# A decode step of attention and gMLP: the last K pair loaded in two pieces, and x's load placed after the first Exp in the program's text

## The chip, the cores and the metric

The kernel runs on one core of one Trainium2 chip. Its time is the device time of one execution in microseconds (us). "The span" is the profile's time from the first to the last instruction of one execution; the run time is 1.7 to 2.2 us longer, because it includes what happens before and after.

The engines have short names: PE multiplies matrices, DVE and ACT do vector and scalar work, and SP here does nothing but issue DMAs (copies between device memory and on-chip memory). Sixteen DMA engines share each large copy. A DMA reports its landing on a semaphore, a counter that other engines can wait for.

## The reference, cut to what matters

One token, batch 1, all arrays bf16. The first part is attention with layer norm and a residual, and the second is a gated MLP with layer norm and a residual.

```python
q = layernorm(x) @ wq                      # 640 -> 32 heads x 192
k, v = the last 4096 keys of k_cache, v_cache   # 32 heads, 192 each: 2 x 50 MB
p = softmax(q . k * 192 ** -0.5)           # per head
h = x + (p @ v) @ wo                       # 6144 -> 640
z = gelu(layernorm(h) @ w_in)              # 640 -> 1536
z1, z2 = z[:768], layernorm(z[768:])
out = h + (z1 * (w_sp * z2 + b_sp)) @ w_out    # 768 -> 640
```

Nearly all of the 119 MB that must be read are K and V. The arithmetic is small, so this is a kernel for streaming memory.

## The kernel before

SP issues all large loads in the order of a plan, into six buffers of 3 MB, as soon as a buffer is free. Each K or V load is one pair of heads; there are 16 pairs. The very last K pair and V pair come in four pieces, so that work on them can begin before all has landed.

```python
def dma_pair(kind, cache, t_):
    t = kvp.tile([P, KVE], BF16, tag="kv", name=kind + "_t")
    cuts = LAST if t_ == NP - 1 else (0, J)    # LAST = (0, J/2, 3J/4, 7J/8, J)
    for a, b in zip(cuts, cuts[1:]):
        load(t[:, None, a * Dh:b * Dh], pair_keys(cache, t_, a, b))
...                                            # the plan: wq, K, V, the last wo, w_in, w_out
nc.scalar.dma_start(out=x_row[:], in_=A_x[0])  # x, on ACT's queue
issue()                                        # wq and the first K loads, on SP's queue
nc.scalar.dma_start(out=wsp_bf[:, 0:1], ...)   # w_sp, two bytes
nc.scalar.dma_start(out=wsp_bf[:, 1:2], ...)   # b_sp, two bytes
nc.scalar.activation(out=warm[:], in_=warm[:], func=ACT.Exp)   # brings in the Exp table
...
```

The end of the program:

```python
project(NQ - 2, oT)                            # the last wo tile but one
...
values(NP - 1, vt, 0, LAST[-3])                # last V pair: 64 small matmuls, in pieces
fold(rows_sb)
values(NP - 1, vt, LAST[-3], LAST[-2])
...
values(NP - 1, vt, LAST[-2], J)
scaled(NP - 1)                                 # "the last V cast": PSUM to SBUF
columns(oT, NQ - 1, 1)
project(NQ - 1, oT)                            # needs the last wo tile
nc.vector.tensor_scalar(out=h_pc[:], ...)      # "the h cast": h is complete
...                                            # layer norm, w_in, gelu, layer norm, gate, w_out
nc.vector.tensor_copy(out=o_sb[:], in_=orow)   # "the output cast"
nc.sync.dma_start(out=out[...], in_=o_sb[0::32, :])   # the store
```

The framework gives each DMA in turn the next of eight DMA semaphores, 0 to 7. A DMA is not issued until the one eight before it, on the same semaphore, has landed. At the end of the program, SP waits for all semaphores, two to a wait, in a fixed order.

Of the kernel before, what the change touches and what calls it, by code (L numbers as in the profile page):

```python
# [9 lines left out]
F32 = mybir.dt.float32  # L10
I32 = mybir.dt.int32
ALU = mybir.AluOpType
ACT = mybir.ActivationFunctionType
# [3 lines left out]
def kernel(  # L17
# [14 lines left out]
    nc = tc.nc  # L32
    P = nc.NUM_PARTITIONS
# [4 lines left out]
    J = W // HALF  # L38
# [6 lines left out]
    NP = H // 2  # L45
# [10 lines left out]
    def load(out, in_):  # L56
        eng = nc.sync
        eng.add_instruction(mybir.InstDMACopy(  # L58
            name=nc.get_next_instruction_name(), mode="Copy", queue="qSPDynamicHW",
            ins=eng.lower_ap_dma(in_, for_custom_bir_dma=True),  # L60
            outs=eng.lower_ap_dma(out, for_custom_bir_dma=True)))

    def pair_keys(cache, t, a, b):
        h0 = 4 * (t // 2) + t % 2
        k0 = Sk - W + a * HALF
        return cache[0, h0:h0 + 3:2, k0:k0 + (b - a) * HALF, :].rearrange("h (p j) d -> p h (j d)", p=HALF // 2)
# [7 lines left out]
    LAST = (0, J // 2, 3 * J // 4, 7 * J // 8, J)  # L74
# [8 lines left out]
    const = ctx.enter_context(tc.tile_pool(name="const", bufs=1))  # L83
# [22 lines left out]

    def dma_pair(kind, cache, t_):
        t = kvp.tile([P, KVE], BF16, tag="kv", name=kind + "_t")
        cuts = LAST if t_ == NP - 1 else (0, J)
        for a, b in zip(cuts, cuts[1:]):  # L110
            load(t[:, None, a * Dh:b * Dh], pair_keys(cache, t_, a, b))
        tiles[(kind, t_)] = t
# [12 lines left out]
    for t_ in range(2):  # L125
        plan.append(("kv", lambda t=t_: dma_pair("k", A_k_cache, t)))
    for t_ in range(NP):
        if t_ + 2 < NP:
            plan.append(("kv", lambda t=t_ + 2: dma_pair("k", A_k_cache, t)))
        if t_ % 2 == 1 and t_ < NP - 1:  # L130
            plan.append(("wo", lambda q=t_ // 2: dma_wo(q)))
        plan.append(("kv", lambda t=t_: dma_pair("v", A_v_cache, t)))
# [8 lines left out]
    def issue():  # L141
        while plan and live[plan[0][0]] < limit[plan[0][0]]:
            kind, go = plan.pop(0)
            live[kind] += 1
            go()

    def free(kind, n=1):
        live[kind] -= n
        issue()

    nc.scalar.dma_start(out=x_row[:], in_=A_x[0])
    issue()
    wsp_bf = const.tile([1, 2], BF16)
    nc.scalar.dma_start(out=wsp_bf[:, 0:1], in_=B_w_sp[0:1])
    nc.scalar.dma_start(out=wsp_bf[:, 1:2], in_=B_b_sp.rearrange("(o n) -> o n", o=1))

    warm = const.tile([P, 1], F32)
    nc.vector.memset(warm[:], 0.0)
    nc.scalar.activation(out=warm[:], in_=warm[:], func=ACT.Exp)
    ones_bf = const.tile([P, P], BF16)  # L160
    nc.vector.memset(ones_bf[:], 1.0)
    ones_f = const.tile([P, P], F32)
# [501 lines left out]
```

## Time and profile before

| | before |
|---|---|
| time, median of 3 runs (lowest to highest) | 286.69 us (286.62 to 286.86) |
| span of the profiled execution | 285.0 us |
| mean granted PE clock in it | 0.818 |
| main DMA queue, share of 16 engines | 97.7% |

The queue is the limit over the whole span.

The end of the chain of waits, in order of time (start, duration, what), says what ended last:

```profile
260.53 13.82 DMA wo_t<-in_A_wo_dram
...
280.97 1.01 PE sc_ps L632 x18
282.01 0.33 DVE o_sb L635
```

So the last wo tile, landing at 274.35, ends the streaming part, and small steps follow until the output cast at 282.01. The timeline of the same stretch (start, duration, engine, line, operation, and what ended the idle time before) has the last V pair's matmuls, the last V cast and the store:

```profile
269.52 1.60 PE L404 MATMUL pv_176<-v_t,E_125 128*2 128x192 bf16 x44
...
272.51 0.26 DVE L429 CAST ol_1866<-pv_176 128x96 bf16<-128x96 f32 x1 [0.33 <-PE pv_176 L404]
...
274.39 0.53 PE L480 MATMUL attn_ps<-o_1882,wo_t 128*128 128x1 bf16 x15 [0.23 <-DMA wo_t<-in_A_wo_dram]
...
282.36 0.63 SPq L636 DMA_DIRECT2D out_dram<-o_sb  x1
```

The start of the program, also from the timeline:

```profile
0.74 0.51 ACTq L151 DMA_DIRECT2D x_row<-in_A_x_dram  x1
...
1.89 1.28 ACT L159 ACT_TABLE_LOAD   x1 [1.89 <-issue]
...
2.17 0.29 PE L239 MATMUL sm_ps<-ones_bf,x_row 1*128 1x1 bf16 x5 [2.17 <-DMA x_row<-in_A_x_dram]
...
6.49 0.16 DVE L243 COPY x_pc<-sm_ps 128x5 f32<-128x5 f32 x1
```

x is issued at 0.74, PE has it at 2.17, and DVE takes the result only at 6.49, because it builds constants before. The wait list of SP has the wait for the store at the end of the program (in total, times, longest):

```profile
SPq L659 <- DMA out_dram<-o_sb: 0.9, 1, 0.9
```

### The profile page before, as it was taken

The numbers are of one execution on the slowest core, as the hardware profiler recorded it, in microseconds if no ns is written. First come the engines' busy times: TensorE is split into PE (matmuls) and PEld (weight loads), VectorE is DVE, ScalarE is ACT, GpSimd is POOL, SyncE is SP. The second block draws the span as 40 slices with busy tenths as digits, with TensorE's granted clock in tenths as the row PEclk, the third lists the DMA queues.
The fourth block names the chain that finished last, engine by engine and source line by source line (L and its number), as shares of the span: only waits on it lengthen the run. The fifth ranks groups of instructions, "written<-read, shape, count | busy, mean of one in ns | idle before, by whom it ended". The sixth has DMA issues, their size and how long they took to land.

```text
span 285.0 us, 3082 instructions
## 1 busy us (share of the span) xinstructions
PE 170.7 (60%) x1134; PEld 67.3 (24%) x1134; DVE 212.3 (74%) x289; ACT 64.1 (22%) x316; POOL 2.3 (1%) x10
## 2 busy tenths in 40 slices
PE   0329938474686259807772476535771876764864
PEld 0103413121132013302220122112320322321453
DVE  7300088989999995999699949996699849995343
ACT  2001237411441224014401440143101010202311
POOL 3000000000000000000000000000000000000000
PEclk9999996889599755985698759956896679999595
DMA  8999999999999999999999999999999998999993
GB/s 331 435 407 428 441 429 400 443 465 428 414 414 437 441 441 428 414 452 421 435 441 442 428 430 441 409 448 435 423 428 443 441 437 384 459 421 423 402 401 140
DMA packets 5565, 119.54 MB, mean 419 GB/s; under 512 B 1005, under 2 KB 2286, under 8 KB 2990
## 3 DMA queue, kind: packets, MB, share of 16 engines
q1 hardware_dynamic: 5544, 119.35, 97.7%
q8 instruction: 9, 0.15, 0.2%
q14 instruction: 6, 0.05, 0.0%
q10 hardware_dynamic: 6, 0.00, 0.0%
HBM read 119.34 MB, written 0.00 MB: 419 GB/s over the span
## 4 chain that ended last, share of the span: by engine, by line
DMA 40%; DVE 38%; PE 18%; issue 2%; SPq 1%; ACT 0%; DVEq 0%; ACTq 0%
DVE k_t L318 20%; DMA k_t<-in_A_k_cache_dram 20%; DMA v_t<-in_A_v_cache_dram 9%; PE sc_ps L325 8%; DMA wq_t<-in_A_wq_dram 6%; PE sc_ps L266 5%; DMA wo_t<-in_A_wo_dram 5%; DVE S L311 5%; DVE ob L439 4%; DVE S L332 3%; PE attn_ps L475 1%; SPq L58 1%; PE sm_ps L342 1%; DVE gm L344 1%; DVE m L335 1%
## 5 line engine op out<-in xcount | busy, mean ns | idle before, releaser
L325 PE MATMUL sc_ps<-k_t,ident_bf 128*128 128x512 bf16 x306 | 91.7, 459 | 45.6 <-DVE k_t L318 45.6
L318 DVE TENSOR_TENSOR k_t<-k_t,q_208 128x6144 bf16<-128x6144 bf16 x32 | 107.1, 3350 | 15.0 <-DMA k_t<-in_A_k_cache_dram 14.6
L325 PEld LDWEIGHTS <-ident_bf 128*128 128x128 bf16 x306 | 32.8, 112 | 96.0 <-issue 62.3
L308 ACT ACTIVATE k_t<-k_t 128x192 bf16<-128x192 bf16 x112 | 38.8, 347 | 34.1 <-DVE k_t L318 34.1
L332 DVE TENSOR_REDUCE S<-sc_ps 128x32 f32<-128x512 f32 (+1 forms) x32 | 21.8, 682 | 4.4 <-PE sc_ps L325 4.4
L266 PE MATMUL sc_ps<-wq_t,xn_128 128*128 128x512 bf16 x60 | 18.3, 467 | 10.3 <-DMA wq_t<-in_A_wq_dram 7.9
L308 ACT ACTIVATION_READ_ACCUMULATOR k_t<-k_t 128x1 f32 x112 | 20.9, 186 | 0.0
L311 DVE TENSOR_REDUCE S<-k_t 128x16 f32<-128x3072 bf16 x6 | 20.1, 3345 | 0.0
L274 DVE COPY sp_f<-sm_ps 128x2 f32<-128x2 f32 x1 | 0.2, 159 | 26.1 <-PE sm_ps L272 26.1
L361 ACT ACTIVATE E_125<-S,bias 128x64 bf16<-128x64 f32 x12 | 4.2, 360 | 46.3 <-DVE bias L351 46.3
L361 ACT ACTIVATE E_127<-S,bias 128x64 bf16<-128x64 f32 x10 | 3.5, 360 | 48.0 <-DVE bias L351 48.0
L361 ACT ACTIVATE E_126<-S,bias 128x64 bf16<-128x64 f32 x10 | 3.5, 362 | 42.9 <-DVE bias L351 42.9
L266 PEld LDWEIGHTS <-xn_128 128*128 128x128 bf16 x60 | 6.7, 112 | 21.6 <-issue 14.6
L268 ACT ACTIVATE q_208<-sc_ps 128x512 bf16<-128x512 f32 x6 | 3.6, 597 | 29.8 <-PE sc_ps L266 29.8
L344 DVE TENSOR_REDUCE gm<-sm_ps 2x1 f32<-2x128 f32 x16 | 4.5, 279 | 7.2 <-PE sm_ps L342 7.2
L414 PE MATMUL pv_174<-v_t,E_127 128*8 128x512 bf16 (+1 forms) x72 | 7.9, 489 | 3.1 <-DMA v_t<-in_A_v_cache_dram 3.1
L414 PE MATMUL pv_176<-v_t,E_126 128*8 128x512 bf16 (+1 forms) x72 | 7.3, 459 | 2.3 <-DMA v_t<-in_A_v_cache_dram 2.3
L414 PE MATMUL pv_176<-v_t,E_125 128*8 128x512 bf16 (+1 forms) x48 | 5.6, 509 | 1.1 <-DMA v_t<-in_A_v_cache_dram 1.1
L414 PE MATMUL pv_174<-v_t,E_125 128*8 128x512 bf16 (+1 forms) x72 | 6.2, 425 | 0.0
L414 PEld LDWEIGHTS <-E_127 128*8 128x8 bf16 (+1 forms) x120 | 3.4, 89 | 8.3 <-issue 6.4
L414 PEld LDWEIGHTS <-E_126 128*8 128x8 bf16 (+1 forms) x120 | 3.4, 86 | 7.6 <-issue 5.2
L414 PE MATMUL pv_176<-v_t,E_127 128*8 128x512 bf16 (+1 forms) x48 | 5.0, 472 | 0.2 <-DMA v_t<-in_A_v_cache_dram 0.2
(242 smaller groups left out, 148.4 us busy)
## 6 DMA issues: line engine op xcount, KB each, us to landing
k_t<-in_A_k_cache_dram SPq DMA_DIRECT2D x15, 3072.0 KB, 27.8
v_t<-in_A_v_cache_dram SPq DMA_DIRECT2D x15, 3072.0 KB, 30.6
wq_t<-in_A_wq_dram SPq DMA_DIRECT2D x5, 1536.0 KB, 14.1
wo_t<-in_A_wo_dram SPq DMA_DIRECT2D x7, 960.0 KB, 19.2
k_t<-in_A_k_cache_dram SPq DMA_DIRECT2D x1, 1536.0 KB
v_t<-in_A_v_cache_dram SPq DMA_DIRECT2D x1, 1536.0 KB
w_in_sb<-in_B_w_in_dram SPq DMA_DIRECT2D x2, 576.0 KB, 14.6
wo_t<-in_A_wo_dram SPq DMA_DIRECT2D x2, 480.0 KB, 13.5
```

The lines of the kernel that those rows point to most:

```text
L58: eng.add_instruction(mybir.InstDMACopy(name=nc.get_next_instruction_name(), mode="Copy", queue="qSPDynamicHW", ins=eng.lower_ap_dma(in_, ...
L266: nc.tensor.matmul(psv, lhsT=xn2[:, c, a, :], rhs=wc[:, gq:gq + 4, a, w0:w0 + P], start=(c == 0 and a == 0), stop=(c == DC - 1 and a == 1))
L268: nc.scalar.activation(out=q2f[:, gq:gq + 4, w0:w0 + P], in_=psv, func=ACT.Copy, scale=scale)
L308: nc.scalar.activation(out=k3[:, j, :], in_=k3[:, j, :], func=ACT.Copy, accum_out=S[:, j:j + 1])
L311: nc.vector.tensor_reduce(out=st[t]["S"][:, J - JS:J], in_=products(t)[:, J - JS:J, :], axis=AX.X, op=ALU.add)
L318: nc.vector.tensor_tensor(out=kc, in0=kc, in1=q2[:, t:t + 1, :].to_broadcast([P, JC, Dh]), op=ALU.mult)
L325: nc.tensor.matmul(psv, lhsT=ident_bf[:], rhs=products(t)[:, j0:j1, n * g:(n + 1) * g], start=(n == 0), stop=(n == Dh // g - 1))
L332: nc.vector.tensor_reduce(out=S[:, j0:j1], in_=st[t]["ps"][ch], axis=AX.X, op=ALU.add)
L344: nc.vector.tensor_reduce(out=gm[:], in_=mT[0:2, 0:P], axis=AX.X, op=ALU.max)
L361: nc.scalar.activation(out=E[:, :, a], in_=S[:], func=ACT.Exp, bias=bias[:, a:a + 1], accum_out=zq[q][:, a, b:b + 1])
L414: nc.tensor.matmul(pv[p0:p0 + 2 * n, :].rearrange("p (k r i) -> p k r i", k=n, r=32), lhsT=E[:, j0:j0 + n, :].rearrange("p j a -> p (j a)" ...
L439: nc.vector.tensor_reduce(out=ob[:, i0:i0 + ni], in_=flat.rearrange("p (k r i) -> p i r k", k=n, i=ni), axis=AX.X, op=ALU.add)
```

## The change

The change has two parts. The last K pair comes in two halves instead of four pieces. That is two DMAs fewer, so every later DMA, and with it the store, moves to another semaphore. The waits at the end stand in a fixed order, so the semaphore decides how many waits still follow once the store has landed. Secondly, x is issued in the program's text after the Exp activation that brings the table in, and the wq loads are issued first, so that they should have the DMA engines to themselves.

```diff
     def dma_pair(kind, cache, t_):
         t = kvp.tile([P, KVE], BF16, tag="kv", name=kind + "_t")
-        cuts = LAST if t_ == NP - 1 else (0, J)
+        cuts = (0, J) if t_ < NP - 1 else LAST if kind == "v" else (0, J // 2, J)
...
+    issue()
+    warm = const.tile([P, 1], F32)
+    nc.vector.memset(warm[:], 0.0)
+    nc.scalar.activation(out=warm[:], in_=warm[:], func=ACT.Exp)
     nc.scalar.dma_start(out=x_row[:], in_=A_x[0])
-    issue()
     wsp_bf = const.tile([1, 2], BF16)
     nc.scalar.dma_start(out=wsp_bf[:, 0:1], in_=B_w_sp[0:1])
     nc.scalar.dma_start(out=wsp_bf[:, 1:2], in_=B_b_sp.rearrange("(o n) -> o n", o=1))
-
-    warm = const.tile([P, 1], F32)
-    nc.vector.memset(warm[:], 0.0)
-    nc.scalar.activation(out=warm[:], in_=warm[:], func=ACT.Exp)
```

## The prediction

> **What bounds the kernel now.** The DMA engines. The page gives the main DMA queue 97.7% of 16 engines' span. In the packet records a 49,152-byte packet takes 1.815 us, and an engine starts its next packet as the last ends, from about 2.1 to 281 us. So the time is start of the first load + bytes of the slowest engine + tail. In the chain of waits the last wo tile lands at 274.35; 7.7 us of small steps follow up to the output cast (282.01). The last w_out load lands at 281.61, just when the last matmuls want it: compute and DMA end together. The store is issued at 282.36 and lands at 284.01.
>
> **What the change does.**
>
> 1. *Exit.* SP ends with five semaphore waits in fixed order, two semaphores each, then a drain. Before, the store is on DMA semaphore 1, in the second wait; that one lasts 0.914 us, and three more follow, 0.063 us apart. With two DMAs fewer, the built program puts the store on semaphore 7, in the fifth wait; the others pass while it is in flight. Gain 3 x 0.063 = **0.19 us**, all critical. The load whose landing the store's issue waits for stays the same (third w_in piece, long landed).
>
> 2. *Last K pair in two pieces.* Packets of 24,576 bytes take 0.913 us, of 12,288 bytes 0.461 us: per engine about 0.04 us are lost in the three smaller pieces. Gain about **0.05 us** (estimate). The second half is multiplied at once anyway. Later loads are issued some us sooner into a queue with over 10 us of backlog: nothing gained.
>
> 3. *x behind the table load.* The load takes 1.28 us, as the Trainium skill says (ScalarE: Activation LUTs, What ACT_TABLE_LOAD costs). The x issue moves from 0.74 to about 2.1-2.3, when wq packets already fill the engines. The skill (DMA: Bandwidth & Descriptors, Queues, rings and completion order) says an engine switches queues only at packet boundaries; this trace agrees: the two-byte w_sp load, issued at 1.28, moved at 4.60 and wrote its semaphore at 6.43, one wq packet later. So x lands at about 6.8 (6.4 to 8.7) instead of 2.2; its copy in DVE moves from 6.49 to about 7.1, the first projection matmul from 9.9 to about 10.6 (up to 12.6). Free: the last wq part lands at 21.85 and only 8 matmuls (3.7 us) can run before it, so there are about 8 us of slack. K's first issue now waits for the first wq part (7.3 instead of 4.0), 14 us before the queue runs dry: free. In return wq has no x or w_sp issues beside it: its first packets start at 2.07-2.15 on eight engines, 2.55-2.82 on seven, 3.33 on one. I expect the slowest engine **0.1 us** earlier (a guess, the least certain term).
>
> **Sum.** 0.19 + 0.05 + 0.1 = 0.34 us: 286.69 becomes **286.35 us**, range 285.9 to 286.7. Chances: faster by over 2% 0.005, within 2% 0.99, slower by over 2% 0.005.
>
> **What would show it.** Step 1: SP's long wait is the last of the five; store landing to end of span is 0.19 us shorter. Step 2: two K issues of 1,536 KB. Step 3: x issued after the table load, landing past 6 us, first projection matmul later, last wq landing unchanged to 0.2 us; earlier first wq packets.
>
> **What would make it wrong.** Engines do not end together: at wo's landing the slowest is 0.8 us behind the median, because 15 instruction fetches (0.3 to 1.0 us each) fall on single engines. Should their places or the start offsets shift, that is worth 0.5 us either way, more than the change. Or x lands so late (past 14 us) that PE delays the queries.

## More of the kernel before

From the profile's page come the main DMA queue (packets, MB, share of the 16 engines' span), the division of the chain of waits by engine, and the granted PE clock in 40 slices of the span, where 9 means 90% of full speed or more and 5 about half.

```profile
PEclk9999996889599755985698759956896679999595
...
q1 hardware_dynamic: 5544, 119.35, 97.7%
...
DMA 40%; DVE 38%; PE 18%; issue 2%; SPq 1%; ACT 0%; DVEq 0%; ACTq 0%
```

PE is done with V at about 272.5, then takes some small steps and the half of wo that has landed, and waits 0.23 us for the last wo tile, which lands at 274.35. PE has slack there, but not much. The windows show how it comes about; the columns are the stretch, its length, the busy time of PE, PE's weight loads, DVE, ACT and POOL, the granted PE clock, the DMA share and GB/s.

```profile
264.00:268.00 4.00, 3.27 (x28) 1.40 (x31) 0.93 (x4) 2.20 (x4) 0.00 (x0) 0.50 0.95 402
268.00:272.00 4.00, 4.00 (x85) 2.63 (x79) 2.74 (x4) 0.48 (x1) 0.00 (x0) 0.74 0.98 404
272.00:276.00 4.00, 2.65 (x75) 2.10 (x66) 1.14 (x7) 0.50 (x3) 0.00 (x0) 1.00 1.05 402
```

From 268 to 272, PE is busy in all of the 4.00 us.

## The result, and the profile after

| | before | after |
|---|---|---|
| median of 6 runs of the same rounds (lowest to highest) | 286.87 us (286.62 to 286.99) | 286.55 us (286.28 to 287.24) |
| ratio, with its 95% interval | | 0.9995 (0.9982 to 1.0008) |
| the profiled execution: run time, span | 286.91, 285.0 | 287.00, 285.2 |

A ratio is the mean time of one kernel's fast runs over the mean of the other's of the same rounds, so it isn't quite the ratio of the medians in the table. The interval holds 1.0: this comparison can't tell the two kernels apart. The changed kernel was run beside the kernel before in four sets of rounds altogether. The differences of the means were -0.15, -0.23, -0.70 and -0.14 us; of the medians, -0.31, -0.49, -0.50 and -0.43 us. Over all of these runs (23 after, 38 before, on several chips), the lowest were 286.28 and 286.60 and the highest 288.27 and 288.68. So both kernels scatter over some 2 us, several times what is to be explained. The mean of the four differences is -0.30 us, give or take 0.25 (an estimate of a 95% interval, from the scatter of these runs): the changed kernel is probably a little faster. Of the four sets alone, only one (e13 below) has an interval that leaves 1.0 out.

One execution of each was profiled, and that of the changed kernel happened to be one of its slower ones: 287.00 against 286.91. This is useful, because it shows what the scatter is made of. The page's lines of the changed kernel:

```profile
PEclk9999979799699557975898559955796879989575
...
q1 hardware_dynamic: 5384, 119.35, 97.6%
...
DVE 41%; DMA 37%; PE 18%; issue 2%; SPq 1%; ACT 0%; DVEq 0%; ACTq 0%
```

There are 160 packets fewer for the same bytes, as there should be. The slices of the clock differ. The chain of waits ends in another way:

```profile
234.31 30.34 DMA v_t<-in_A_v_cache_dram
264.69 1.87 PE pv_174 L413 x12
...
269.80 1.88 PE pv_176 L403 x18
...
274.20 0.92 PE attn_ps L479 x30
...
281.37 1.00 PE sc_ps L631 x23
282.39 0.32 DVE o_sb L634
```

There is no wait for wo any more: from the landing of the V pair before the last at 264.64 on, the chain runs through PE. In the timeline the first 44 matmuls recorded for the last V pair, begun at the same time as before (269.48 against 269.52), take 2.20 us instead of 1.60, and the last V cast comes 0.56 us later:

```profile
269.48 2.20 PE L403 MATMUL pv_176<-v_t,E_125 128*2 128x192 bf16 x44
...
273.07 0.26 DVE L428 CAST ol_1864<-pv_176 128x96 bf16<-128x96 f32 x1 [0.94 <-PE pv_176 L403]
...
282.75 0.63 SPq L635 DMA_DIRECT2D out_dram<-o_sb  x1
```

The windows give the reason in the clock column: 0.59 from 268 to 272 instead of 0.74, and 0.84 from 272 to 276 instead of 1.00.

```profile
264.00:268.00 4.00, 3.31 (x31) 1.42 (x34) 0.97 (x4) 2.19 (x4) 0.00 (x0) 0.56 0.95 401
268.00:272.00 4.00, 4.00 (x72) 2.42 (x64) 2.78 (x4) 0.48 (x1) 0.00 (x0) 0.59 1.00 413
272.00:276.00 4.00, 2.91 (x77) 2.48 (x77) 0.78 (x5) 0.50 (x3) 0.00 (x0) 0.84 1.05 402
```

At the start, the order in the program's text did not do what it seems to say:

```profile
0.73 1.28 ACT L154 ACT_TABLE_LOAD   x1 [0.73 <-PEq L647]
...
0.91 0.50 ACTq L155 DMA_DIRECT2D x_row<-in_A_x_dram  x1
...
2.37 0.29 PE L238 MATMUL sm_ps<-ones_bf,x_row 1*128 1x1 bf16 x5 [2.37 <-DMA x_row<-in_A_x_dram]
...
6.48 0.16 DVE L242 COPY x_pc<-sm_ps 128x5 f32<-128x5 f32 x1
```

The table load runs from 0.73 to 2.02, and x is issued at 0.91, in the midst of it. Its packet even moves before any of wq: from 1.79 to 2.03 in the packet records, where the first wq packet starts at 2.07, though wq was issued first. x reaches PE 0.20 us later than before, and DVE takes the result at the same time as before. At the end, SP's wait for the store is shorter, though the store takes as long to land (1.64 us after its issue, 1.65 before):

```profile
SPq L658 <- DMA out_dram<-o_sb: 0.7, 1, 0.7
```

The trace's records of SP's last instructions show the order of the waits (start and duration in us; the numbers in brackets are the DMA semaphores that a wait covers, where they could be told):

```
before                                   after
282.359 0.632 store issued               282.745 0.632 store issued
283.053 0.028 wait (3, 2)                283.438 0.028 wait
283.117 0.914 wait (4, 1)  <- store      283.503 0.028 wait
284.009       store has landed           283.564 0.028 wait
284.065 0.028 wait (5, 0)                283.628 0.028 wait
284.129 0.028 wait                       284.383       store has landed
284.191 0.028 wait                       284.399 0.028 wait (7, ...)  <- store
284.256 0.013 drain                      284.464 0.013 drain
284.320 0.007 drain, the last            284.528 0.007 drain, the last
```

The end of the program went as the prediction said: before, three waits still follow after the landing; after the change, none does. From the landing to the last drain it is 0.311 us before and 0.145 after.

The two profiled executions can now be balanced. The h cast comes 0.19 us later (275.246 against 275.053), and from there to the output cast it takes 0.19 us more (7.147 against 6.953). The exit is 0.17 shorter, and the time outside the span is 0.12 shorter (1.78 against 1.90). The sum is about 0.09 us, the difference of their run times. So in this pair PE at half speed took 0.39 us; against it stand 0.17 at the exit, which the change explains, and 0.12 outside the span, which nothing here explains.

### The profile page after: what moved, and what is told of

It reads as the page before. It is cut to its first block, busy times and chain, and to the rows that moved or that the text cites. A ratio compares the mean times of both kernels' runs of the same rounds, so it can differ in the third digit from the quotient of the medians.

```text
span 285.2 us, 3077 instructions
## 1 busy us (share of the span) xinstructions
PE 172.3 (60%) x1134; PEld 67.9 (24%) x1134; DVE 212.3 (74%) x289; ACT 64.1 (22%) x316; POOL 2.3 (1%) x10
## 4 chain that ended last, share of the span: by engine, by line
DVE 41%; DMA 37%; PE 18%; issue 2%; SPq 1%; ACT 0%; DVEq 0%; ACTq 0%
DVE k_t L317 22%; DMA k_t<-in_A_k_cache_dram 20%; DMA v_t<-in_A_v_cache_dram 11%; PE sc_ps L324 7%; DMA wq_t<-in_A_wq_dram 7%; DVE S L310 5%; PE sc_ps L265 5%; DVE ob L438 4%; DVE S L331 4%; PE pv_174 L413 1%; PE attn_ps L474 1%; PE sm_ps L341 1%; SPq L58 1%; PE pv_176 L403 1%; DVE gm L343 1%
## 5 line engine op out<-in xcount | busy, mean ns | idle before, releaser
L324 PE MATMUL sc_ps<-k_t,ident_bf 128*128 128x512 bf16 x306 | 93.0, 464 | 47.0 <-DVE k_t L317 47.0
L265 PE MATMUL sc_ps<-wq_t,xn_128 128*128 128x512 bf16 x60 | 17.2, 444 | 10.4 <-DMA wq_t<-in_A_wq_dram 7.9
L413 PE MATMUL pv_174<-v_t,E_127 128*8 128x512 bf16 (+1 forms) x72 | 7.9, 488 | 3.0 <-DMA v_t<-in_A_v_cache_dram 3.0
L413 PE MATMUL pv_176<-v_t,E_126 128*8 128x512 bf16 (+1 forms) x72 | 8.1, 492 | 0.7 <-DMA v_t<-in_A_v_cache_dram 0.5
L413 PE MATMUL pv_176<-v_t,E_125 128*8 128x512 bf16 (+1 forms) x48 | 5.8, 521 | 0.9 <-DMA v_t<-in_A_v_cache_dram 0.9
L413 PE MATMUL pv_174<-v_t,E_125 128*8 128x512 bf16 (+1 forms) x72 | 6.2, 424 | 0.0
L413 PE MATMUL pv_176<-v_t,E_127 128*8 128x512 bf16 (+1 forms) x48 | 5.0, 474 | 1.8 <-DMA v_t<-in_A_v_cache_dram 1.8
```

The source lines that it names most:

```text
L265: nc.tensor.matmul(psv, lhsT=xn2[:, c, a, :], rhs=wc[:, gq:gq + 4, a, w0:w0 + P], start=(c == 0 and a == 0), stop=(c == DC - 1 and a == 1))
L324: nc.tensor.matmul(psv, lhsT=ident_bf[:], rhs=products(t)[:, j0:j1, n * g:(n + 1) * g], start=(n == 0), stop=(n == Dh // g - 1))
L413: nc.tensor.matmul(pv[p0:p0 + 2 * n, :].rearrange("p (k r i) -> p k r i", k=n, r=32), lhsT=E[:, j0:j0 + n, :].rearrange("p j a -> p (j a)" ...
```

## The experiments

The theory to start with was the prediction's own: a gain at the exit through the semaphore's place (A), little from the pieces (B), and a gain from a freer start of the wq loads (C). A fourth was added: the scatter comes from the PE clock near the end (D). Its rival was the one named in the prediction: the scatter comes from the lag between the 16 DMA engines (E).

In the diffs below, "after" stands for the changed kernel, and "before" for the kernel before, from which the lines are edited. The kernel before was run in the same rounds each time. The chips differ from one set of rounds to the next.

### Set 1: each half of the change alone, more pieces, and the changed kernel again

e1 takes the two pieces alone, e2 the moved x alone. e3 cuts K into five pieces, so that the store's semaphore moves the other way. e4 is the changed kernel.

```diff
# e1: before, with
-        cuts = LAST if t_ == NP - 1 else (0, J)
+        cuts = (0, J) if t_ < NP - 1 else LAST if kind == "v" else (0, J // 2, J)
# e2: before, with the moved x of the change
# e3: before, with
+        cuts = (0, J) if t_ < NP - 1 else LAST if kind == "v" else LAST[:-1] + (15 * J // 16, J)
```

> The kernel before with the last K pair in two pieces, x where it was. The store is then on semaphore 7. Theory (the exit is all that the change gains, the rest is scatter from the TensorE clock's phase in the tail): store landing to SP's drain 0.15 us as in the changed kernel (before 0.32), time 286.65 us or 0.15 us under the kernel before, like the whole change. Rival A (moving x cost what the exit gained, so the parts are +0.2 and -0.3): 0.3 us under the kernel before. Rival B (the exit is hidden behind other engines' barrier): store landing to end of span equal to before.

> Only x is moved behind the table load; the K pair stays in four pieces and the store on semaphore 1. Theory: x is issued at about 0.9 us, during the table load, and lands at about 2.4; store landing to SP's drain 0.32 us as before; time equal to before within 0.1 us. Rival A: slower than before by 0.15 us or more, with a later last wq landing (21.94 in the changed kernel, 21.85 before).

> The kernel before with the last K pair in five pieces: the store falls on semaphore 2, in the first of SP's five waits, the worst place. Theory: store landing to SP's drain 0.38 us (0.32 before, 0.15 in the changed kernel), time 0.06 us over the kernel before. Rival B: landing to end of span as before.

> The changed kernel again, for its scatter and a second trace. Theory: store landing to SP's drain 0.15 us again, but the time from the last wo landing to the store's issue differs from the first trace (8.45 us there, 8.0 in the kernel before) because the half-speed windows of the TensorE clock fall elsewhere; runs between 286.2 and 287.3 us, mean 286.65. Rival C (the change itself makes the tail 0.4 us longer): the tail is 8.4 us again and half speed covers 274.7 us to the end again.

| kernel | median (lowest to highest), us | ratio (95%) | landing of the store to SP's last drain | waits that follow the store's |
|---|---|---|---|---|
| before, 11 runs | 287.09 (286.60 to 287.93) | | 0.311 | 3 |
| e1, two pieces | 286.84 (286.35 to 287.58) | 0.9988 (0.9968 to 1.0007) | 0.145 | 0 |
| e2, x moved | 287.47 (287.01 to 288.53) | 1.0011 (0.9991 to 1.0032) | 0.311 | 3 |
| e3, five pieces | 287.06 (286.97 to 288.57) | 1.0004 (0.9983 to 1.0026) | 0.376 | 4 |
| e4, the change | 286.60 (286.37 to 288.27) | 0.9995 (0.9969 to 1.0020) | 0.146 | 0 |

The time from landing to drain follows the place of the store's semaphore, here and in all 18 traces (to 0.001 us); moving x does not touch it. A is shown for SP's part. From landing to the end of the span it is 1.001 us before and in e2, 0.835 after the change and in e1 and e4, so the gain is not hidden behind the other engines. But e3 has 1.152 and not 1.066: there DVE's last instruction comes late and ends the span 0.09 us later, for a reason that was not tested. Between three and four waits there are 0.065 us, but the whole step from three to none is 0.166 and not three times 0.063: in the records above, the blocked wait ends 0.022 us after the landing before (283.117 + 0.914 against 284.009) and 0.044 us after it in the changed kernel (284.399 + 0.028 against 284.383). Those 0.022 us are missing from the gain. In e3, where the store's semaphore is also the second of the two in its wait, it is 0.023 us, and 0.043 or 0.044 in e6, e1 and e14, where it is the first; why was not tested.

The whole times say less. Taken together as a two by two table of means (287.21, 286.89, 287.57, 286.99), the two pieces are worth -0.45 us and the moved x +0.23, but within one kernel the runs differ by over 1 us and no interval leaves 1.0 out. No gain from moving x can be seen, and C has no support; nor has the rival that the move costs time by a later wq (the last wq landing is 21.86 in e2 and 21.85 before).

### Set 2: x behind the table load for certain, one piece, and less work for PE

In e5, ACT writes one element of x's buffer after the Exp, so that the DMA really has to wait for the table load. e6 loads the last K pair whole, which puts the store on semaphore 6, in the fourth wait; it ran once. e7 and e8 take away much of PE's work from the ninth pair on: eleven of twelve matmuls of each contraction cover only four keys. The result is wrong (the comparison with the reference passed all the same, so this is below its tolerance). My theory D then said that the clock falls under load, so that with less work PE would keep full speed.

```diff
# e5: after, with
     nc.scalar.activation(out=warm[:], in_=warm[:], func=ACT.Exp)
+    nc.scalar.copy(out=x_row[0:1, 0:1], in_=warm[0:1, 0:1])
     nc.scalar.dma_start(out=x_row[:], in_=A_x[0])
# e6: before, with
-        cuts = LAST if t_ == NP - 1 else (0, J)
+        cuts = (0, J) if t_ < NP - 1 else LAST if kind == "v" else (0, J)
# e7: before, e8: after, each with
-            nc.tensor.matmul(psv, lhsT=ident_bf[:], rhs=products(t)[:, j0:j1, n * g:(n + 1) * g],
+            jn = j1 - j0 if t < 8 or n == 0 else 4
+            nc.tensor.matmul(psv[:, 0:jn, :], lhsT=ident_bf[:], rhs=products(t)[:, j0:j0 + jn, n * g:(n + 1) * g],
```

> The changed kernel, but x's load really waits for the table load: a one-element ScalarE copy into the x row, behind the first Exp, must finish before it. x is issued at about 2.3 us. Theory (the prediction's arithmetic for step 3 was right, only its premise that the issue stands behind the table load was wrong): x's packet waits for one wq packet and its semaphore write for another, x reaches PE at 6.8 us (6.4 to 8.7), first projection matmul at 10.6 (up to 12.6) instead of 9.9; the last projection matmul and the time unchanged to 0.2 us. Wq's first packets begin at 2.07 us with the last engine near 3 us as before if the other issues do not delay them; if they do, the last engine begins 0.1 us or more earlier. Rival: x lands by 4 us, since a small packet is served between two large ones and its semaphore at once.

> The kernel before with the last K pair in one piece: the store falls on semaphore 6, the first semaphore of SP's fourth wait, so one wait follows. Theory: store landing to SP's last drain 0.21 us (0.145 in the fifth wait, 0.311 in the second, 0.376 in the first). Rival B (only fewer DMAs matter, not the place): 0.14 us or less.

> The kernel before with nearly no contraction work on PE from pair 8 on: eleven of twelve matmuls cover 4 keys instead of 32 (wrong result on purpose), all loads and the instruction count the same. Theory (the scatter and the lost gain come from half-speed windows of the TensorE clock while PE works between the last V tiles and the last wo): no half-speed window between 258 and 275 us, last V cast by 272.2 us, the runs within 0.3 us of each other, near 286.4 us. Rival (scatter has another cause, the DMA engines): runs still spread over 1 us, from 286.5 to 288.

> The same with the changed kernel. Theory: with the scatter gone the change shows its own size: 0.17 us (the exit) to 0.25 us (with two DMAs fewer) under the run with the kernel before, landing to end of span 0.835 against 1.001 us. Rival: no difference, or more than 0.3 us.

| kernel | median (lowest to highest), us | ratio (95%) | mean PE clock, profiled execution |
|---|---|---|---|
| before, 11 runs | 287.02 (286.63 to 287.19) | | |
| e5 | 287.41 (286.39 to 288.15) | 1.0013 (0.9995 to 1.0031) | 0.822 |
| e6, one run | 288.45 | not timed | 0.798 |
| e7 | 288.81 (288.53 to 289.68) | 1.0070 (1.0058 to 1.0082) | 0.708 |
| e8 | 288.38 (287.06 to 289.15) | 1.0048 (1.0030 to 1.0066) | 0.721 |

The start of e5:

```profile
2.26 0.19 ACT L155 CAST x_row<-warm 1x1 bf16<-1x1 f32 x1
...
2.48 0.60 ACTq L156 DMA_DIRECT2D x_row<-in_A_x_dram  x1
...
7.13 0.27 PE L239 MATMUL sm_ps<-ones_bf,x_row 1*128 1x1 bf16 x5 [7.13 <-DMA x_row<-in_A_x_dram]
```

With a true dependence the arithmetic of step 3 comes out: x is at PE at about 7.1 (6.8 was forecast), the first projection matmul is at 10.85 (10.6 forecast), and the last projection matmul ends no later than before (it starts at 35.37, against 35.78). The delay is free, as forecast. What was missing in the change was the dependence itself. The gain that it was to bring is missing in e5 too: its wq packets start on the 16 engines between 2.07 and 2.86 us, those of the changed kernel, whose x came early, between 2.07 and 2.87.

e6 has its store's wait fourth, with one wait after it, and 0.207 us from landing to drain: the series of places now reads 0.376, 0.311, 0.207, 0.145. That its single run was 1.4 us longer than before is no verdict on one piece. Its trace has PE at half speed from 266.2 to the end.

e7 and e8 went against me. PE had less to do, and its clock fell to 0.71 on average; both kernels became slower, by 1.9 us (e7) and 1.4 us (e8) in the means. A window of e8 shows the lower clock: PE is busy all the time from 268 to 272, at half speed.

```profile
268.00:272.00 4.00, 4.00 (x68) 2.11 (x64) 2.60 (x6) 1.31 (x3) 0.00 (x0) 0.50 0.99 410
```

They did not show the size of the change either: their means differ by 0.55 us, and from landing to the end of the span e8 has 0.918 us and e7 1.296, where 0.835 and 1.001 had been expected, because one of DVE's last instructions again comes late and lengthens it by 0.08 and 0.30 us. From landing to drain they have 0.146 and 0.312, as they should.

So D stood with the wrong sign: it is too little work, not too much, that makes the clock fall. The Trainium skill states it (TensorE: Matmul & The Clock Gate, Part 1: The HAM clock gate): half rate is the default, a window of about 3.4 us of activity brings full rate, idle windows bring half rate back, and the window runs on its own, not in step with the kernel. The trace agrees: in the clock records of all traces here, changes are multiples of 3.4 us apart, and the half-speed stretch before the last V cast begins at 263.3, 264.5, 264.8, 265.1, 265.8 or 266.2 in different executions of nearly the same program. Before each such stretch PE waits for V with little to do. Windows of 3.41 us can be laid on the grid of the clock's own changes: in the last one before the stretch PE is busy for 1.38 us in the kernel before (259.9 to 263.3), 0.22 in the changed kernel, and 0.21 to 1.38 in all ten executions of the last table below. Over all 18 traces, before 272 us, each of the 210 falls to half speed follows a window in which PE is busy for at most 1.80 us, and each of the 206 rises one with at least 2.61 us. Busy time is not the whole rule: full speed was also kept after windows with 1.36 us, and e6 stayed at half speed after one that PE's records fill (268.2 to 271.6).

### Set 3: idle matmuls that keep PE busy

If the clock near the end hides the change, then enough work for PE before that place must remove the scatter, and the same work elsewhere must not. e10 (before) and e11 (after) have 27 additional matmuls on data that is never used, at pairs 14 and 15. e12 (after) has the same 27 at pairs 5 and 6. e13 is the changed kernel.

```diff
+    def keep_warm(n):
+        spare = bank()
+        for _ in range(n):
+            nc.tensor.matmul(spare, lhsT=ident_bf[:], rhs=q2[:].rearrange("p t d -> p (t d)")[:, 0:512], start=True, stop=True)
...
+        if t >= NP - 2:          # e12: t in (5, 6)
+            keep_warm(5)
...
+        if t == NP - 1:          # e12: t == 6
+            keep_warm(6)
...
+    keep_warm(11)                # after the last exps; e12: at the end of pair 6
```

> The kernel before with 27 idle matmuls (128x512, results unused) in PE's waits at pairs 14 and 15 and before the last full V tile. New theory, after the light kernels had more half speed (mean clock 0.71) instead of less: half speed follows idle windows of 3.41 us on a grid that does not start with the kernel; a busy PE keeps full speed. Then no half-speed window lies between 258 and 272 us, the last V cast is at 272.5 us or earlier, the h cast at 275.1 or earlier, and the runs lie within 0.5 us of each other near 286.6 us, mean below the kernel before's. Rival (the window's place has nothing to do with PE's work; or the idle matmuls get in the way): last V cast after 273 us, runs spread over 1 us as before.

> The same 27 idle matmuls in the changed kernel. Theory: near 286.4 us, runs within 0.5 us, 0.17 to 0.3 us under the kernel before with the same matmuls, since the scatter that hid the change is gone; landing to end of span 0.835 us. Rival: no difference between the two.

> Control: the changed kernel with the same 27 idle matmuls at pairs 5 and 6, far from the tail. Theory: scatter and mean as the changed kernel without them (286.3 to 288.3, mean about 286.9). Rival (the matmuls help by shifting instruction fetches, not by the clock): as the warm kernel.

> The changed kernel in the same rounds, for comparison: 286.3 to 288.3 us, mean about 286.8; landing to drain 0.145 us; last V cast later than 272.5 us just where a half-speed window reaches past 270 us.

| kernel | median (lowest to highest), us | ratio (95%) |
|---|---|---|
| before, 10 runs | 287.16 (286.86 to 288.68) | |
| e10, warm before | 287.00 (286.82 to 287.23) | 0.9995 (0.9983 to 1.0008) |
| e11, warm after | 286.88 (286.74 to 287.16) | 0.9990 (0.9977 to 1.0002) |
| e12, warm elsewhere, after | 287.19 (287.03 to 287.95) | 1.0004 (0.9991 to 1.0017) |
| e13, the change | 286.66 (286.45 to 286.93) | 0.9981 (0.9967 to 0.9995) |

Windows of e11 in the critical stretch:

```profile
264.00:268.00 4.00, 3.23 (x46) 1.55 (x45) 1.98 (x6) 2.64 (x5) 0.00 (x0) 1.00 0.95 400
268.00:272.00 4.00, 2.60 (x82) 2.13 (x81) 2.06 (x3) 0.03 (x1) 0.00 (x0) 1.00 0.98 405
```

PE is at full speed throughout and needs 2.60 us for about as many matmuls (82) as took it all of the 4.00 us at 0.74 (85, before) and 0.59 (72, after). In e11 full speed holds from 252.0 to 272.5 and in e10 from 252.6 to 273.0. In e12, the control, half speed is back from 263.3 to 270.1. The last V cast comes at 272.26 in e10 and 272.27 in e11, as forecast (272.5 or earlier), and at 272.47 in e12. The runs of e10 and e11 lie within 0.41 and 0.42 us, those of e12 within 0.92, and those of the kernel before in the same rounds within 1.82. e13, which has no idle matmuls, was quiet in these rounds too (0.48), so the range of one set is weak evidence; the traces carry the argument.

Warm against warm, the change is worth -0.16 us in the means (286.88 against 287.04). But the times that I had forecast for the warm kernels (286.6 and 286.4) were missed, and e11's mean is 0.23 us above that of e13, which has no idle matmuls. In e11's trace the clock falls at 272.5 and the small steps after it run at half speed, so that the output cast (282.04) comes 0.21 us later than w_out's landing (281.43) would have allowed by the second rule below. e12's mean is 0.64 us above e13's; 0.36 of it lies outside the span and isn't explained.

### Set 4: many pieces, and the idle matmuls carried on to the end

e14 cuts the last K pair into ten pieces, six more than before. The store is then again on semaphore 7 (six more and two fewer differ by eight), so A alone says that it exits as well as the changed kernel. e15 and e16 add 20 more idle matmuls between the last steps, to hold full speed until some 278 us. e17 is the changed kernel.

```diff
# e14: before, with
+        cuts = (0, J) if t_ < NP - 1 else LAST if kind == "v" else (0, 32, 36, 40, 44, 48, 52, 56, 60, 62, 64)
# e15: e10, e16: e11, each with
-    values(NP - 1, vt, 0, LAST[-3])
+    keep_warm(2)
+    values(NP - 1, vt, 0, J // 2)
+    keep_warm(4)
+    values(NP - 1, vt, J // 2, LAST[-3])
...                             # and 4, 5 (of 128 columns), 3 and 2 more in the steps after
```

> The kernel before with the last K pair in ten pieces: the store is on semaphore 7 again, but SP has six DMAs more than before, not two fewer. Theory (place of the store's semaphore alone sets the exit inside the span): landing to SP's drain 0.145 us, landing to end of span 0.84. Outside the span: 1.83 us if it follows the semaphore, another value (before 1.94, five pieces 1.73) if it follows how many instructions SP has. Rival for the exit (fewer DMAs matter): landing to drain 0.31 us or more.

> The kernel before with the 27 idle matmuls and 20 more between the last V pieces and in the waits of the MLP. Theory: full speed from 255 us to 278 or beyond, store issued 0.1 to 0.3 us sooner after the last wo landing than with 27[...], runs within 0.5 us, near 286.9. Rival: the extra matmuls stand before critical ones and cost 0.2 us or more.

> The same in the changed kernel. Theory: 0.17 to 0.28 us under e15_warm_end_before, near 286.65, at or under the changed kernel's mean, with less scatter. Rival: no difference to e15_warm_end_before.

> The changed kernel again in the same rounds: lowest 286.3 to 286.5, mean 286.6 to 287.0, outside the span 1.83 us, landing to end of span 0.835 us.

| kernel | median (lowest to highest), us | ratio (95%) | landing to last drain |
|---|---|---|---|
| before, 11 runs | 287.10 (286.79 to 287.34) | | |
| e14, ten pieces | 289.63 (289.03 to 289.81) | 1.0085 (1.0072 to 1.0098) | 0.145 |
| e15, warm to the end, before | 287.07 (286.98 to 287.16) | 0.9999 (0.9986 to 1.0012) | 0.311 |
| e16, warm to the end, after | 286.95 (286.56 to 287.01) | 0.9993 (0.9981 to 1.0004) | 0.145 |
| e17, the change | 286.67 (286.37 to 288.22) | 0.9994 (0.9978 to 1.0011) | 0.146 |

e14 confirms A once more and refutes "more pieces do no harm". SP's timeline in e14, and the same lines of the kernel before:

```profile
213.25 31.87 SPq L58 DMA_DIRECT2D k_t<-in_A_k_cache_dram  x10
245.22 0.54 SPq L58 DMA_DIRECT2D wo_t<-in_A_wo_dram  x1
```

```profile
213.53 3.50 SPq L58 DMA_DIRECT2D k_t<-in_A_k_cache_dram  x4
230.95 0.49 SPq L58 DMA_DIRECT2D wo_t<-in_A_wo_dram  x1
```

From the sixth piece on, each needs a semaphore whose earlier DMA is still in the queue, and SP stands there until it has landed: these pieces are issued at 225.77, 233.03, 240.28, 243.94 and 244.52. The next load is issued 14 us late. The queue, which is the bottleneck, runs dry. In the packet records of the kernel before, never fewer than 16 packets are under way from 236 to 258; in e14 it is down to 8 at about 245.9, and from 245 to 247 it is 12.8 on average. That is some 0.4 us of all engines (an estimate: 3.2 of 16 for 2 us). The packets of wo after it take up to 2.08 us instead of 1.14, and the small pieces cost time as well: the second half of the pair takes 63.8 engine-us instead of 59.5, 0.27 us on each engine. The last w_out load lands at 282.95, 1.34 us after that of the kernel before (281.61), and in this trace the store also takes 2.68 us to land instead of 1.65, for a reason that was not tested. For these two executions (289.03 and 286.91) the sum is 1.37 to the output cast, 1.03 for the store, less 0.17 at the exit and 0.12 outside the span: 2.11 us of 2.12.

The time outside the span is 1.82 us on average in e14, as it would be if it followed the semaphore; but e12, with the DMAs and the semaphores of the changed kernel, has 2.18, so it does not follow the semaphore alone.

e15 and e16 missed what I expected: the clock still fell at about 273. In e15 the store was issued 8.33 us after the last wo landing, not sooner than in e10 (8.23 in its trace). Small matmuls with gaps between them did not hold it, and neither kernel is faster than its shorter version. Warm against warm, the change is worth -0.21 us (286.868 against 287.074). No kernel beats the changed kernel beyond its scatter (e1, the two pieces alone, can't be told from it).

### What all the traces say together

For each profiled execution the ends of four things can be read: the half-speed stretch that covers the last V matmuls, the last V cast, the landing of the last wo tile, and that of the last w_out load. The rows are sorted by the end of half speed.

| profiled execution | half speed ends | last V cast | wo landed | h cast | w_out landed | output cast | run time |
|---|---|---|---|---|---|---|---|
| e4, the change | 268.5 | 272.11 | 274.00 | 274.71 | 281.39 | 281.78 | 286.49 |
| e17, the change | 268.7 | 272.19 | 274.07 | 274.79 | 281.35 | 281.75 | 286.37 |
| before | 270.1 | 272.51 | 274.35 | 275.05 | 281.61 | 282.01 | 286.91 |
| e13, the change | 270.2 | 272.58 | 274.38 | 275.10 | 281.76 | 282.16 | 286.76 |
| e3 | 270.9 | 272.86 | 274.29 | 275.05 | 281.56 | 282.19 | 287.03 |
| after, the change | 271.3 | 273.07 | 274.30 | 275.25 | 281.62 | 282.39 | 287.00 |
| e2 | 271.3 | 272.99 | 274.07 | 275.17 | 281.33 | 282.32 | 287.36 |
| e1 | 271.6 | 273.36 | 274.56 | 275.53 | 281.83 | 282.68 | 287.29 |
| e5 | 272.6 | 273.75 | 274.47 | 275.91 | 281.74 | 283.05 | 287.68 |
| e6 | not before the end | 274.41 | 274.12 | 276.63 | 281.46 | 283.77 | 288.45 |

Two rules fit the rows to 0.1 us. The h cast comes 0.70 us after wo has landed or 2.17 us after the last V cast, whichever is later. The output cast comes 0.40 us after w_out has landed or, where all steps between run at half speed, 7.14 us after the h cast, whichever is later. In e4, e17, e13 and before, the DMA has the last word both times; there PE ran a part of the steps after the h cast at full speed, so that the 7.14 does not apply (it would be up to 0.18 us too late). In the other six PE has the last word at the output cast, and they are longer by what PE is behind. For these ten executions this decides between D and E, and both take part: the landings of wo and w_out differ by 0.56 and 0.50 us from row to row and are E's part of the scatter; the output cast differs by 2.0 us, and the last V cast, which follows the end of half speed, accounts for the rest. The changed kernel stands in the table at 268.5 and at 271.3, so it is the place of the window and not the change that differs. The longest executions of the changed kernel (288.22, 288.27) were timed but not traced; that they are like e6 is plausible and not shown. The mean granted clock does not settle it: both have 0.804, but there are runs of the changed kernel with 0.800 and 0.801 at 286.60 and 286.66.

## Why the prediction was right or wrong

The time of 286.35 us lay 0.2 us from the measured median, and the range held it, but the forecast gain of 0.34 us was not resolved in these rounds (0.15 us in the means, ratio 0.9995, 0.9982 to 1.0008). The step that failed is step 3, with the 0.1 us that was built on it: x did not wait for the table load (issued at 0.91, not 2.1 to 2.3), and wq did not start earlier.

- **What bounds the kernel: right, but not complete.** The DMA queue, and then a tail where "compute and DMA end together". The trace shows how fine this balance is. "Together" was read off one execution; in others PE ends up to 1.9 us after the DMA (e6: 283.77 against 281.46 + 0.40). The clock that decides this stood in the page and was not read.

- **Step 1, the exit: mechanism right, size a little off.** The store is on semaphore 7 in the fifth wait, and 0.166 us are gained (0.311 to 0.145), not 0.19. The term mis-sized is "3 x 0.063": the blocked wait also ends sooner or later after the landing by its form. Four places of the semaphore (e3; before; e6; e1 and e14) show it. Besides, the time outside the span is 1.83 us on average for the changed kernel and 1.94 for the kernel before, a further 0.11 us that no step foresaw. It isn't explained: e3, with more DMAs and the longest exit, has 1.73, e2 has 2.00, and e12, with the changed kernel's DMAs, 2.18.

- **Step 2, the K pieces: not settled.** In the packet records the second half of the pair takes 58.4 engine-us in one piece and 59.5 in three, 0.07 us on each engine, so the pieces do cost about what was forecast. Whether it reaches the end can't be seen, since 0.05 us is smaller than what can be resolved: the landing of the last w_out load scatters by 0.5 us between traces of kernels with the same pieces. Two K issues were seen, as forecast.

- **Step 3, x behind the table load: wrong, and this is the step that failed.** "The x issue moves from 0.74 to about 2.1-2.3" assumed that ACT's queue would hold the DMA back until the table load is done. It was issued at 0.91, while the load ran. "x lands at about 6.8" was 2.4, "first projection matmul from 9.9 to about 10.6" stayed at 9.91. With a true dependence (e5) these figures came out at 7.1 and 10.85, so the arithmetic was sound and the premise was not. What was forecast of K's first issue did come (7.42 against 7.3), but for it the wq loads merely had to come first on SP.

- **"I expect the slowest engine 0.1 us earlier": not seen, and part of the failed step.** The last engine's first wq packet started between 2.86 and 3.76 in the ten traces with moved x and between 2.54 and 3.33 in the eight without, 3.05 on average in both. The last w_out load landed at 281.54 us on average in ten traces with moved x and at 281.57 in seven without (e14 left out). Nothing was gained, whether x came early or, in e5, late.

- **"What would make it wrong": half right.** The lag of single DMA engines is there and shifts the landings by up to 0.5 us, as it says. The other source, PE's clock in the last 20 us, is not named; in e5 and e6 it is the larger. In the traces of the changed kernel alone PE ends up to 0.37 us after the DMA (282.39 against 281.62 + 0.40), about as much as the landings of w_out differ there (281.35 to 281.76); over the ten traces of the table, up to 1.9 us.

So the change gives 0.17 us at the exit. The changed kernel has, on average, 0.11 us less outside the span, 0.28 us together; that the change is the cause of the second part isn't shown. The differences of the medians (0.31 to 0.50) and the comparison of warm kernels (0.16 and 0.21) stand on either side of this. That the forecast of 0.34 comes near it is luck and no confirmation, as two of its three terms weren't seen in the time.

## What to carry to other kernels

When a change is worth a tenth of a per cent, find first what makes the executions of one kernel differ; here the table of last arrivals (clock, PE, DMA) says more, from ten traces, than some sixty runs' times. An order in the program's text is no order in time: x's issue, written behind the table load, came at 0.91 us, in the midst of it, and at 2.48 when it had a true dependence on what follows the load. So give a load that should come late such a dependence. Count the DMAs behind the last one and see where its semaphore stands among the final waits: the place can be chosen by the number of pieces, as long as SP need not wait for a semaphore before it can issue them (e14).

## What the Trainium skill lacked or had wrong

- ScalarE: Activation LUTs (What ACT_TABLE_LOAD costs) gives 1283 ns for the load and 1380 ns of drain. The traces agree on the load (1.28 us), but in the changed kernel the activation begins at 2.03, 0.01 us after the load ends at 2.02, so here no such drain was seen. The page does not say that DMA issues on ACT's queue go on during the load (x issued at 0.91, load from 0.73 to 2.02); the prediction failed on this.
- TensorE: Matmul & The Clock Gate (Part 1: The HAM clock gate) holds in its rule and its window (changes multiples of 3.4 us apart; e7, e8 slower with less work, e10, e11 at full speed with more). It calls the ramp's penalty less than 1% of a typical span and advises against fitting a count of slow matmuls. Here the last V cast moved from 272.11 to 274.41 with the end of half speed, and PE ended up to 1.9 us after the DMA (e6), 0.7% of the time: within the page's figure, and more than the change that was to be judged.
- DMA: Bandwidth & Descriptors (Queues, rings and completion order): a switch of queues only at packet boundaries agrees with w_sp, two bytes issued at 1.28 and moved at 4.60. In the kernel before, w_sp's semaphore came at 6.43, one wq packet after its data; in e5, x's semaphore came at 6.48 directly after its data at 6.43. I found nothing in that section on what decides between the two, and it was not tested.
- Runtime: NRT & Kernel Launch (Instruction fetch mechanics) calls the cost of refilling instructions mostly hidden. Whether the engines that execute them waited was not looked at; but the fetches take time of the same 16 DMA engines: nine of 16,384 bytes took 0.88 to 1.04 us each and six of 8,192 bytes 0.31, and while one ran in the stream of K and V, 15 packets of the main queue were under way instead of 16. The page gives no such cost.
- No page that I read has the cost of the place of the last DMA's semaphore among the final waits: 0.376, 0.311, 0.207 and 0.145 us from landing to drain with four, three, one and no waits behind it.
